# Attention and two mixers on one Trainium2 core: the second chunk's channel units and token products go ahead of the first's last ones, and the first batches' loads and k^T v products are spread

## The chip, the cores and the metric

The program runs on one core of one Trainium2 chip. The time is device microseconds (us) of one execution; three runs of the kernel before gave 1113.26 to 1115.82 us, median 1114.48. Engines: PE (TensorE) does matmuls, DVE (VectorE) and ACT (ScalarE) elementwise work, POOL (GpSimd) small work and some DMA issues, SP (SyncE) issues nearly all DMAs. On each engine instructions run in the order in which they were issued.

## The reference

Eight batches, 8 heads, 576 tokens, head size 64, so the model width is 512. Cut to what matters:

```python
kv  = einsum('bhsd,bhse->bhde', k, v)            # k^T v, no softmax
out = einsum('bhsd,bhde->bhse', q, kv)
x   = out / rms(out) * g_norm                    # heads side by side: [b, 576, 512]

theta = x @ w_theta                              # mixer 1
y = w_tok_r @ (x * cos(theta)) + w_tok_i @ (x * sin(theta))   # over tokens
u = x + y
x = u + relu(u @ w_ch)

h = relu(x^T @ w_tok1) @ w_tok2                  # mixer 2, over tokens: 576 -> 256 -> 576
u = x + h^T
return u + relu(u @ w_ch1) @ w_ch2               # 512 -> 1536 -> 512
```

## The kernel before, in words

**Precision.** Most fp32 products are made of three fp16 products (`mm3`, lines 104 to 106): each operand is split into a high part (ACT) and a low part (DVE: the value minus the high part). Some weights come as 64-bit numbers; `decode` (lines 150 to 158: one ACT copy and three DVE integer operations) makes them fp32 before the split.

**Units.** The tokens are in two chunks, columns 0 to 255 (chunk 0) and 256 to 575 (chunk 1). The work of a batch is cut into units, each one stretch of PE work with ACT and DVE work behind it. In the names the first digit is the chunk, the second the output tile.

- `kv` (L327): k^T v of a batch in two halves (token rows 0 and 1; rows 2, 3 and 4), in the bank kvp; the second half is followed by a copy into kvbd. Each half, when done, issues the loads of the same rows of the next batch's k and v (`load_kv`, L292), since they use the freed buffers.
- a0 to a4, or n0 and n1 when they belong to the batch after next (`attend`, L347): q times kvbd into the bank po, then the norm (ACT L358, DVE L360, POOL, DVE L365) and x. For later batches x is split and transposed by a DMA (L383).
- r0 to r4 (`rotate`): x times w_theta into pt, then L416, L420, sine and cosine (L423 to L425), L428 multiplies by x, L432 and L435 split the result into zh and zl. r4 covers the last 64 tokens; its part of zh comes by a DMA transpose from zt (L480). The buffer cs, which L416 to L435 use, exists twice.
- M00 to M13 (`mix`): 27 matmuls each over zh, zl and wm into py.
- C00 to C13 (`channel`): 12 matmuls each into pr (256 or 320 columns), then DVE L532 adds relu to R, ACT L533 and DVE L540 split the result into xs, and after each second unit SP transposes xs into xt (L544).
- H00 to H11 (`token1`): x^T times w_tok1 into the bank ph; H0x uses chunk 0's xt (6 matmuls), H1x chunk 1's (8). Behind each H1x `split_relu` makes hh and hl.
- T00 to T13 (`token2`): hh, hl times w2 into pu, then DVE L575 adds to R.

**Order.** `run` issues a list of units in program order; a dictionary says what is issued beside (behind) a unit: "a2", "r0", "l" (load the heads of the batch after next), "w" (a step of a weight's load and decode), "k" (a half of `kv`). `go` issues a unit's PE work and lets every unit under way do its next step, so that ACT and DVE work is dealt out behind later units. The list `STEADY` holds the order of batches 2 to 5. `placed`, `lead` and `urgent` say how the scheduler may move instructions. Batch 1 has its own lists because the token units of batch 0 run inside it; batches 6 and 7 have others. After all batches comes the MLP of mixer 2 (`mlp`).

**Start.** Batch 0's q, k, v and w_theta are loaded, then wm of chunk 0 (`mix_weights(0)`), the heads of batch 1, and after batch 0's rotations wm of chunk 1 (`mix_weights(1)`) and w_ch. The weight tiles use staging memory, for wm the buffers that later hold zh and zl. All k^T v products of batches 1 to 7 are made in the start, between batch 0's rotations and beside its M units, before the memory of k and v is given to the decoded weights of the token mixer (w1, w2).

Of the kernel before, what the change touches and what calls it, by code (L numbers as in the profile page):

```python
# [11 lines left out]
F32 = mybir.dt.float32  # L12
# [7 lines left out]
P = 128  # L20
# [8 lines left out]
def attn_mixer_kernel(  # L29
# [4 lines left out]
    nc = tc.nc  # L34
# [4 lines left out]
    NR = S // P  # L39
# [14 lines left out]

    const_ctx, mix_ctx, tok_ctx, front_ctx, start_ctx, stash_ctx = (ExitStack() for _ in range(6))
    const = const_ctx.enter_context(tc.tile_pool(name="const", bufs=1, side="left"))
    zp = mix_ctx.enter_context(tc.tile_pool(name="zp", bufs=2, side="left"))
    mp = mix_ctx.enter_context(tc.tile_pool(name="mp", bufs=1, side="left"))
    fp = front_ctx.enter_context(tc.tile_pool(name="fp", bufs=1, side="right"))
    kp = start_ctx.enter_context(tc.tile_pool(name="kp", bufs=2, side="right"))  # L60
    stg = start_ctx.enter_context(tc.tile_pool(name="stg", bufs=3, side="left"))
# [46 lines left out]

    ident = const.tile([P, P], F32, name="ident")
    make_identity(nc, ident)  # L110
# [185 lines left out]
    for b, o in enumerate(batches):  # L296
        o.b, o.zh, o.kv = b, None, []

# [247 lines left out]
    def token1(o, part, j):  # L546
        b = o.b
        if j == 0 and part == 0:
            o.ph = [bank(f"ph{b}{i}") for i in range(KJ)]
            o.hh = tk[0].tile([P, KJ, DM], F16, tag="hh", name=f"hh{b}", bufs=1)  # L550
            o.hl = tk[0].tile([P, KJ, DM], F16, tag="hl", name=f"hl{b}")
        js = slice(j * P, (j + 1) * P)
        ph = o.ph[j].rearrange("p (k d) -> p k d", k=KD)
        xt = o.x2[part].rearrange("p (k r) d -> p r k d", k=KD)
        low = xt.shape[1] - 2
        for r in range(2):
            wr = 2 * part + r
            nc.tensor.matmul(ph, w1[0][:, wr, js], xt[:, r], start=wr == 0, stop=False)
            nc.tensor.matmul(ph, w1[0][:, wr, js], xt[:, low + r], start=False, stop=False)
            nc.tensor.matmul(ph, w1[1][:, wr, js], xt[:, r], start=False, stop=False)  # L560
        if part:
            nc.tensor.matmul(ph, w1rh[:, js], xt[:, 2], start=False, stop=False)
            nc.tensor.matmul(ph, w1rl[:, js], xt[:, 2], start=False, stop=True)
            yield
            with urgent():
                split_relu(o.hh[:, j, :], o.hl[:, j, :], o.ph[j])
        yield
# [195 lines left out]
    def go(unit, lead=False):  # L763
        advance()
        next(unit)
        (leading if lead else pending).append(unit)

    def advance():

        for units in (leading, pending):  # L770
            for g in list(units):
                try:
                    next(g)
                except StopIteration:
# [26 lines left out]
    prepare(o)  # L801
    extra += mix_weights(0)
    for r in range(1, NR + 1):
# [20 lines left out]
    def run(units, o, nxt, after, also):  # L824
# [21 lines left out]
    loaded = []  # L846
    STEADY = MIX[:6] + CHANNEL[:2] + MIX[6:] + CHANNEL[2:] + TOKEN1 + TOKEN2
    BESIDE = {
        "M00": "a2", "M01": "a3", "M02": "a4 l w", "M03": "r0", "M11": "r1", "M12": "r2",
        "C03": "r4", "C10": "w", "H01": "r3 w n0", "T01": "n1 w", "T12": "w",  # L850
    }
    for b in range(B):
        loaded.clear()
        if b == 0:
            run(MIX, o, nxt, None, {
                "M00": "k w w w", "M01": "k w w w", "M02": "k a0 w", "M03": "k a1 w", "M10": "k a2 k w", "M11": "a3 k w",
                "M12": "a4 r0 k l", "M13": "r1 k",
            })
            after = loaded[0]
            spare(len(extra))  # L860
            flush()
            start_ctx.close()
            wp.append(stash_ctx.enter_context(tc.tile_pool(name="wp", bufs=2, side="right", reuse_waits="tile")))
            tk.append(tok_ctx.enter_context(tc.tile_pool(name="tk", bufs=1, side="left", reuse_waits="tile")))
            extra += [weight_tile(wp[0], w_tok1, w1, j, DT, SW, "w1") for j in range(NR)]
            src, _ = words(w_tok1)
            extra += [weight(wp[0], w_tok1, src[SM:], SR, DT, w1rh[:SR], w1rl[:SR], SW, "w1r")]
            extra += [weight_tile(wp[0], w_tok2, w2, j, S // 2, SW, "w2", col) for j in range(KJ) for col in range(0, S, S // 2)]
            run(CHANNEL, o, nxt, after, {
                "C00": "r2 w", "C01": "r3 w", "C02": "w", "C03": "r4 w", "C10": "w", "C11": "w", "C12": "w", "C13": "w",  # L870
            })
            spare(len(extra))
# [5 lines left out]
        elif b == 1:  # L878
            run(MIX[:4], o, nxt, None, {})
            run(TOKEN1 + TOKEN2, before, None, nxt, {"T00": "n0", "T02": "n1", "T10": "n2 w", "T12": "n3"})  # L880
            run(MIX[4:6] + CHANNEL[:1], o, nxt, None, {"M10": "a4 l"})
            after = loaded[0]
            run(STEADY[STEADY.index("C01"):], o, nxt, after, {
                "C01": "r0", "M12": "r1", "M13": "r2", "C03": "r4", "C10": "w", "H01": "r3 w n0", "T01": "n1 w", "T12": "w",
            })
# [83 lines left out]
```

## Time and profile before

| | kernel before |
|---|---|
| three runs | 1115.82, 1114.48, 1113.26 us |
| the profiled execution's own time | 1117.14 us |
| its span | 1115.4 us |
| PE busy (matmuls) | 1068.9 us, 96% |
| DVE busy | 813.5 us, 73% |
| ACT busy | 567.6 us, 51% |
| mean granted clock of PE | 0.992 |
| moved by DMA | 126.32 MB, mean 113 GB/s |

The span runs from the first to the last instruction that the profiler saw; the execution's own time has a little before and behind it. Busy time says how long an engine had work in flight; what limits a stretch is read from what ended the idle time in it. A wait is put down to what came last. A granted clock of 1.0 is 2.4 GHz on PE, 0.5 is 1.2 GHz.

### The profile page before, as it was taken

What the parts mean: (1) busy time and instruction counts of PE and PEld (TensorE: products, weight loads), DVE (VectorE), ACT (ScalarE), POOL (GpSimd) and SP (SyncE); (2) the same over time, 40 slices, a digit from 0 to 9 for tenths busy, and PEclk for the clock granted to TensorE, in tenths of its full rate; (3) what the DMA queues carried; (4) which work ended last, traced back from release to release, by engine and by line L of the source; (5) the groups of instructions that cost most, each with busy time, mean ns of one, the idle gap of its engine ahead of it and who ended that gap; (6) DMA issues with size and microseconds to landing.
All of it is one profiled execution on the core that took longest, in us unless ns stands there. A gap on an engine that the chain in (4) does not pass through costs nothing.

```text
span 1115.4 us, 21660 instructions
## 1 busy us (share of the span) xinstructions
PE 1068.9 (96%) x8884; PEld 812.2 (73%) x8884; DVE 813.5 (73%) x1483; ACT 567.6 (51%) x970; POOL 189.7 (17%) x259
## 2 busy tenths in 40 slices
PE   4789989999999999989999999999999999999998
PEld 4467667676766767657777777777777777777776
DVE  5877787889788886888745585848677685758584
ACT  3754654737456464565522544536264544446361
POOL 3203005262443624435000000000000000000000
PEclk9889999999999999999999999999999999999999
DMA  9899447383754837546274702020110102020101
GB/s 302 240 308 287 115 110 183 81 216 99 171 150 106 221 95 170 142 106 141 39 264 103 267 11 75 8 79 1 43 43 29 59 11 76 12 75 1 44 1 43
DMA packets 147859, 126.32 MB, mean 113 GB/s; under 512 B 93296, under 2 KB 123120, under 8 KB 147760
## 3 DMA queue, kind: packets, MB, share of 16 engines
q1 hardware_dynamic: 142384, 104.49, 35.4%
q0 software_dynamic: 5376, 20.45, 5.1%
q8 instruction: 69, 1.13, 0.4%
q14 instruction: 30, 0.25, 0.1%
HBM read 74.25 MB, written 29.88 MB: 93 GB/s over the span
## 4 chain that ended last, share of the span: by engine, by line
PE 63%; DVE 14%; DMA 9%; ACT 6%; issue 2%; POOL 2%; SPq 2%; DVEq 0%; ACTq 0%
PE na L104 4%; PE pa L104 4%; PE pa L106 4%; PE pa L105 4%; PE na L106 4%; PE na L105 4%; DMA xt<-xs 3%; PE py L104 3%; PE py L106 3%; PE py L105 3%; DVE zl L435 2%; PE pc L106 2%; PE pc L105 2%; PE pc L104 2%; PE nc L105 2%
## 5 line engine op out<-in xcount | busy, mean ns | idle before, releaser
L104 PE MATMUL py<-wmh,zh 128*128 128x320 f16 (+1 forms) x576 | 166.4, 289 | 2.6 <-ACT zh L432 2.0
L105 PE MATMUL py<-wml,zh 128*128 128x320 f16 (+1 forms) x576 | 166.3, 289 | 0.0
L106 PE MATMUL py<-wmh,zl 128*128 128x320 f16 (+1 forms) x512 | 147.9, 289 | 1.6 <-DVE zl L435 1.6
L106 PE MATMUL na<-gh,wbl 128*128 128x288 f16 x384 | 109.3, 286 | 0.0
L105 PE MATMUL pa<-o,wah 128*128 128x288 f16 x384 | 109.2, 286 | 0.0
L105 PE MATMUL na<-gl,wbh 128*128 128x288 f16 x384 | 109.1, 286 | 0.0
L104 PE MATMUL pa<-o,wah 128*128 128x288 f16 x384 | 108.4, 286 | 0.0
L106 PE MATMUL pa<-o,wal 128*128 128x288 f16 x384 | 107.8, 286 | 0.0
L104 PE MATMUL na<-gh,wbh 128*128 128x288 f16 x384 | 106.0, 286 | 0.2
L648 DVE TENSOR_TENSOR gl<-sum,gh 128x1152 f16<-128x1152 f32 x48 | 65.1, 1356 | 21.9 <-ACT gh L647 21.9
L105 PEld LDWEIGHTS <-wbh 128*128 128x128 f16 x672 | 65.7, 98 | 17.7 <-issue 1.0
L104 PEld LDWEIGHTS <-wah 128*128 128x128 f16 x672 | 65.8, 98 | 16.6
L105 PEld LDWEIGHTS <-wah 128*128 128x128 f16 x672 | 65.8, 98 | 16.6
L106 PEld LDWEIGHTS <-wbl 128*128 128x128 f16 x672 | 65.7, 98 | 16.6
L106 PEld LDWEIGHTS <-wal 128*128 128x128 f16 x672 | 65.8, 98 | 16.6
L104 PEld LDWEIGHTS <-wbh 128*128 128x128 f16 x672 | 65.7, 98 | 16.6
L106 PE MATMUL pr<-uh,wcl 128*128 128x256 f16 (+1 forms) x256 | 73.1, 286 | 0.3 <-DVE wcl L180 0.3
L105 PE MATMUL pr<-ul,wch 128*128 128x256 f16 (+1 forms) x256 | 73.1, 286 | 0.0
L104 PE MATMUL pr<-uh,wch 128*128 128x256 f16 (+1 forms) x256 | 73.0, 286 | 0.0
L104 PEld LDWEIGHTS <-zh 128*128 128x128 f16 x576 | 57.0, 99 | 19.0 <-ACT zh L432 2.3
L647 ACT ACTIVATE gh<-sum 128x1152 f16<-128x1152 f32 x48 | 55.6, 1158 | 25.5 <-DVE sum L695 25.5
L105 PEld LDWEIGHTS <-zh 128*128 128x128 f16 x576 | 57.0, 99 | 15.7
(309 smaller groups left out, 2866.5 us busy)
## 6 DMA issues: line engine op xcount, KB each, us to landing
c<-u2d SPq DMA_DIRECT2D x32, 288.0 KB, 4.5
out<-c SPq DMA_DIRECT2D x64, 144.0 KB, 1.8
q<-in_q SPq DMA_DIRECT2D x7, 1152.0 KB, 7.0
k<-in_k SPq DMA_DIRECT2D x24, 256.0 KB, 5.7
v<-in_v SPq DMA_DIRECT2D x24, 256.0 KB, 6.1
wa_r<-in_w_ch SPq DMA_DIRECT2D x24, 256.0 KB, 3.6
wb_r<-in_w_ch SPq DMA_DIRECT2D x24, 256.0 KB, 3.8
wad<-wa POOLq DMA_DIRECT2D x24, 224.0 KB, 2.4
```

The costliest lines, as they stand in the source:

```text
L104: nc.tensor.matmul(acc, ah, bh, start=first and i == 0, stop=False, **more)
L105: nc.tensor.matmul(acc, ah, bl, start=False, stop=False, **more)
L106: nc.tensor.matmul(acc, al, bh, start=False, stop=last and i == n - 1, **more)
L435: place(nc.vector.tensor_tensor(zl[:, at, :], cs, zh[:, at, :], ALU.subtract))
L647: nc.scalar.activation(h.hi[:, 3:], h.s, AF.Copy)
L648: nc.vector.tensor_tensor(h.lo[:, 3:], h.s, h.hi[:, 3:], ALU.subtract)
```

## The change

It has three parts.

1. The order of a steady batch. Before: M00 to M11, C00, C01, M12, M13, C02, C03, C10 to C13, H00, H01, H10, H11, T. After: M00 to M13, C00, C01, C10 to C13, C02, C03, H10, H11, H00, H01, T. `token1` may now begin with either chunk: the bank's first product starts it and the second closes it. r4 is issued beside C01, and r3, n0 and n1 beside C03 (before: r4 beside C03, r3 and n0 beside H01, n1 beside T01).
2. The start. wm of chunk 1 is loaded and decoded ahead of k and v of batch 2; `settle` lets the decode of chunk 0 end first. The two halves of k^T v of batch 1 stand beside r3 and r4 of batch 0, and the twelve halves of batches 2 to 7 one behind each of batch 0's eight M units and of C00 to C03. Batch 1's attend units stand beside M00 to M10, its rotations r0 to r2 beside M10 to M12 (before: M12, M13, C00). The memory of k and v (`heads_ctx`) is given back after C03, so w1 and w2 are loaded and decoded beside C10 to C13, two steps a unit.
3. Batch 1 follows the new steady order from M11 on, with r0 to r2 beside M11, M12 and M13.

```diff
-    kp = start_ctx.enter_context(tc.tile_pool(name="kp", bufs=2, side="right"))
+    kp = heads_ctx.enter_context(tc.tile_pool(name="kp", bufs=2, side="right"))
...
-        if j == 0 and part == 0:
+        if o.ph is None:
             o.ph = [bank(f"ph{b}{i}") for i in range(KJ)]
...
+        parts = []
         for r in range(2):
             wr = 2 * part + r
-            nc.tensor.matmul(ph, w1[0][:, wr, js], xt[:, r], start=wr == 0, stop=False)
-            nc.tensor.matmul(ph, w1[0][:, wr, js], xt[:, low + r], start=False, stop=False)
-            nc.tensor.matmul(ph, w1[1][:, wr, js], xt[:, r], start=False, stop=False)
+            parts += [(w1[0][:, wr, js], xt[:, r]), (w1[0][:, wr, js], xt[:, low + r]), (w1[1][:, wr, js], xt[:, r])]
         if part:
-            nc.tensor.matmul(ph, w1rh[:, js], xt[:, 2], start=False, stop=False)
-            nc.tensor.matmul(ph, w1rl[:, js], xt[:, 2], start=False, stop=True)
+            parts += [(w1rh[:, js], xt[:, 2]), (w1rl[:, js], xt[:, 2])]
+        again = j in o.half
+        for i, (w, x) in enumerate(parts):
+            nc.tensor.matmul(ph, w, x, start=not again and i == 0, stop=again and i == len(parts) - 1)
+        o.half.add(j)
+        if again:
             yield
...
+    def settle(units):
+
+        while any(u in pending or u in leading for u in units):
+            advance()
...
     nxt = load_heads(1)
-    for r in range(NR + 1):
+    for r in range(NR - 1):
         go(rotate(o, r))
-        if r == 1:
-            go(kv(nxt, 0))
-            go(kv(nxt, 1))
-        elif r > 1:
-            go(kv(*products.pop(0)))
+    settle(narrow)
+    extra += mix_weights(1)
+    for r in range(NR - 1, NR + 1):
+        spare()
+        go(rotate(o, r))
+        go(kv(nxt, r - NR + 1))
+        spare()
+    spare(len(extra))
     flush()
-    extra += mix_weights(1)
...
-    STEADY = MIX[:6] + CHANNEL[:2] + MIX[6:] + CHANNEL[2:] + TOKEN1 + TOKEN2
+    STEADY = MIX + CHANNEL[:2] + CHANNEL[4:] + CHANNEL[2:4] + TOKEN1[2:] + TOKEN1[:2] + TOKEN2
     BESIDE = {
         "M00": "a2", "M01": "a3", "M02": "a4 l w", "M03": "r0", "M11": "r1", "M12": "r2",
-        "C03": "r4", "C10": "w", "H01": "r3 w n0", "T01": "n1 w", "T12": "w",
+        "C01": "r4", "C12": "w", "C03": "r3 n0 n1 w", "T01": "w", "T12": "w",
     }
...
-                "M00": "k w w w", "M01": "k w w w", "M02": "k a0 w", "M03": "k a1 w", "M10": "k a2 k w", "M11": "a3 k w",
-                "M12": "a4 r0 k l", "M13": "r1 k",
+                "M00": "a0 k", "M01": "a1 k w", "M02": "a2 k w", "M03": "a3 k w", "M10": "a4 k r0 w", "M11": "r1 l k", "M12": "r2 k", "M13": "k",
...
+            run(CHANNEL[:4], o, nxt, after, {"C00": "k", "C01": "r3 k", "C02": "k", "C03": "r4 k"})
+            heads_ctx.close()
...
-            run(CHANNEL, o, nxt, after, {
-                "C00": "r2 w", "C01": "r3 w", "C02": "w", "C03": "r4 w", "C10": "w", "C11": "w", "C12": "w", "C13": "w",
-            })
+            run(CHANNEL[4:], o, nxt, after, {"C10": "w w", "C11": "w w", "C12": "w w", "C13": "w"})
...
-            run(MIX[4:6] + CHANNEL[:1], o, nxt, None, {"M10": "a4 l"})
+            run(MIX[4:5], o, nxt, None, {"M10": "a4 l"})
             after = loaded[0]
-            run(STEADY[STEADY.index("C01"):], o, nxt, after, {
-                "C01": "r0", "M12": "r1", "M13": "r2", "C03": "r4", "C10": "w", "H01": "r3 w n0", "T01": "n1 w", "T12": "w",
+            run(STEADY[STEADY.index("M11"):], o, nxt, after, {
+                "M11": "r0", "M12": "r1", "M13": "r2", "C01": "r4", "C12": "w", "C03": "r3 n0 n1 w", "T01": "w", "T12": "w",
             })
```

What the change does to the order of DVE is shown at the end of batch 3's channel units; before, the last units there are C12 and C13 (pr312, pr313 and their output xs312; zl4 and zt4 are the next batch's rotations):

```order
L532 SCALAR_TENSOR_TENSOR R3_2601<-pr312_4204,R3_2601 128x320
L435 TENSOR_TENSOR zl4_3811<-cs42_4024,zh4_3810 128x2x512
L540 SCALAR_TENSOR_TENSOR xs310_4157<-R3_2601,xs310_4157 128x256
L540 SCALAR_TENSOR_TENSOR xs310_4157<-R3_2601,xs310_4157 128x64
L532 SCALAR_TENSOR_TENSOR R3_2601<-pr313_4223,R3_2601 128x320
L540 SCALAR_TENSOR_TENSOR xs312_4203<-R3_2601,xs312_4203 128x256
L540 SCALAR_TENSOR_TENSOR xs312_4203<-R3_2601,xs312_4203 128x64
L475 TENSOR_TENSOR zt4_4151<-cs44_4150,zt4_4151 128x512
L540 SCALAR_TENSOR_TENSOR xs312_4203<-R3_2601,xs312_4203 128x256
L540 SCALAR_TENSOR_TENSOR xs312_4203<-R3_2601,xs312_4203 128x64
```

The same place on DVE after the change, where C02 and C03 (pr302, pr303, xs302) follow C13:

```order
L532 SCALAR_TENSOR_TENSOR R3_2576<-pr312_4162,R3_2576 128x320
L467 SCALAR_TENSOR_TENSOR cs44_4112<-R4_3418,cs44_4112 128x4x64 x2
L532 SCALAR_TENSOR_TENSOR R3_2576<-pr313_4191,R3_2576 128x320
L435 TENSOR_TENSOR zl4_3811<-cs42_3975,zh4_3810 128x2x512
L540 SCALAR_TENSOR_TENSOR xs312_4161<-R3_2576,xs312_4161 128x256
L540 SCALAR_TENSOR_TENSOR xs312_4161<-R3_2576,xs312_4161 128x64
L532 SCALAR_TENSOR_TENSOR R3_2576<-pr302_4208,R3_2576 128x256
L475 TENSOR_TENSOR zt4_4113<-cs44_4112,zt4_4113 128x512
L532 SCALAR_TENSOR_TENSOR R3_2576<-pr303_4226,R3_2576 128x256
L540 SCALAR_TENSOR_TENSOR xs312_4161<-R3_2576,xs312_4161 128x256
L540 SCALAR_TENSOR_TENSOR xs312_4161<-R3_2576,xs312_4161 128x64
L540 SCALAR_TENSOR_TENSOR xs302_4207<-R3_2576,xs302_4207 128x256 x2
```

The additions L532 of two more channel units now stand ahead of the last two L540, behind which SP transposes xs312 for H10 and H11.

On SP, in the start, the loads before run from batch 1's last rows of k and v on (wm13r and wm17r are single tiles of chunk 1's wm, wmh1 the pairs wm10 and wm11 in one of zh's buffers):

```order
L292 DMA k14_374<-in_k 96x512
L292 DMA v14_376<-in_v 96x512
L205 DMA wm13r_864<-in_w_mix 128x640
L205 DMA wm17r_868<-in_w_mix 128x640
L314 DMA q1_378<-in_q 128x4x576
L316 DMA q1_378<-in_q 128x4x64
L292 DMA k20_459<-in_k 128x512
```

And after, the same stretch of SP's queue:

```order
L292 DMA v14_376<-in_v 96x512
L205 DMA wmh1_456<-in_w_mix 128x2x640 x2
L205 DMA wm13r_646<-in_w_mix 128x640
L205 DMA wm17r_651<-in_w_mix 128x640
L314 DMA q1_378<-in_q 128x4x576
L316 DMA q1_378<-in_q 128x4x64
L292 DMA k20_515<-in_k 128x512
L292 DMA v20_517<-in_v 128x512
L292 DMA k21_519<-in_k 128x512
L292 DMA v21_521<-in_v 128x512
L205 DMA wml1_457<-in_w_mix 128x2x640
```

The two pairs in wmh1, which stood behind all of batch 2's k and v, are now ahead of them, and the pair in wml1 is in their middle. On DVE the decode of these two pairs is issued about r0 and r1 of batch 0 (cs00, cs01) after the change:

```order
L158 SCALAR_TENSOR_TENSOR wm10v_473<-wmh1_456,wm10v_473 128x640
L420 SCALAR_TENSOR_TENSOR cs00_405<-cs00_405,pt00_392 128x512
L156 TENSOR_SCALAR wm11v_532<-wm11v_532 128x640
L214 SCALAR_TENSOR_TENSOR wml_115<-wm08v_390,wmh_114 128x256
L214 SCALAR_TENSOR_TENSOR wml_115<-wm10v_473,wmh_114 128x2x320
L157 SCALAR_TENSOR_TENSOR wm11v_532<-wmh1_456,wm11v_532 128x640
L420 SCALAR_TENSOR_TENSOR cs01_430<-cs01_430,pt01_417 128x512
L69 SCALAR_TENSOR_TENSOR xt04_335<-px4_431,xt04_335 128x512
L158 SCALAR_TENSOR_TENSOR wm11v_532<-wmh1_456,wm11v_532 128x640
L428 TENSOR_TENSOR cs00_405<-cs00_405,x00_240 128x1024
L214 SCALAR_TENSOR_TENSOR wml_115<-wm11v_532,wmh_114 128x2x320
L428 TENSOR_TENSOR cs01_430<-cs01_430,x01_254 128x1024
```

Before, the L420 of cs00 and cs01 and the L428 of cs00 stood next to one another there, and the decode of wm10 came behind zl of r1.

## Rows read from the trace of the kernel before

**Rows 1.** The page's first block: busy us, share of the span, instructions.

```profile
PE 1068.9 (96%) x8884; PEld 812.2 (73%) x8884; DVE 813.5 (73%) x1483; ACT 567.6 (51%) x970; POOL 189.7 (17%) x259
```

**Rows 2.** Waits of PE, whole span: us in total, times, longest.

```profile
PE ph L558 <- DMA xt<-xs: 8.4, 8, 1.3
PE pu L104 <- DVE R L575: 2.3, 5, 0.5
```

**Rows 3.** Waits of PE in 44 to 160 us.

```profile
PE kvp L327 <- DMA v<-in_v: 6.6, 6, 4.0
PE py L104 <- ACT zh L432: 2.0, 1, 2.0
PE py L106 <- DVE zl L435: 1.6, 1, 1.6
PE py L104 <- DMA zh<-zt: 0.7, 1, 0.7
```

**Rows 4.** Windows: length, busy of five engines, PEclk, DMA share, GB/s.

```profile
46.00:115.00 69.00, 62.44 (x828) 47.27 (x825) 51.65 (x88) 36.12 (x67) 10.54 (x10) 0.95 1.02 293
64.00:69.00 5.00, 4.95 (x35) 3.74 (x36) 4.97 (x9) 3.85 (x7) 0.00 (x0) 0.50 1.06 290
144.00:147.00 3.00, 3.00 (x17) 2.13 (x16) 3.00 (x11) 2.09 (x5) 0.00 (x0) 0.52 0.31 87
```

**Rows 5.** Timeline of PE, batch 3: start, duration, instruction, [idle before].

```profile
344.13 0.30 PE L106 MATMUL pr<-uh,wcl 128*128 128x320 f16 x1
344.27 0.38 PE L558 MATMUL ph<-xt,w1h 128*128 128x512 f16 x1
...
349.45 1.05 PE L347 MATMUL po<-kvbd,q 128*128 128x128 f32 x8
351.81 0.39 PE L558 MATMUL ph<-xt,w1h 128*128 128x512 f16 x1 [1.31 <-DMA xt<-xs]
...
355.71 1.06 PE L347 MATMUL po<-kvbd,q 128*128 128x128 f32 x8
356.60 0.27 PE L104 MATMUL pu<-w2h,hh 128*128 128x256 f16 x1
356.71 0.27 PE L105 MATMUL pu<-w2l,hh 128*128 128x256 f16 x1
...
361.84 0.30 PE L104 MATMUL pu<-w2h,hh 128*128 128x320 f16 x1 [0.45 <-DVE R L575]
```

**Rows 6.** Timeline of DVE at the same place in batch 3.

```profile
344.56 1.22 DVE L435 TENSOR_TENSOR zl<-cs,zh 128x1024 f16<-128x1024 f32 x1
...
346.17 0.49 DVE L532 SCALAR_TENSOR_TENSOR R<-pr,R 128x320 f32<-128x320 f32 x1
```

**Rows 7.** Timeline of SP's queue at the same place.

```profile
346.31 3.26 SPq L544 DMA_TRANSPOSE xt<-xs  x2
```

**Rows 8.** Timelines of PE and DVE: batch 1's r3, last matmul, L420, zl.

```profile
126.20 0.38 PE L106 MATMUL pt<-wth,xt 128*128 128x512 f16 x1
...
135.31 0.68 DVE L420 SCALAR_TENSOR_TENSOR cs<-cs,pt 128x512 f32<-128x512 f32 x1
...
141.78 1.23 DVE L435 TENSOR_TENSOR zl<-cs,zh 128x1024 f16<-128x1024 f32 x1
```

**Rows 9.** Timeline of DVE: zl of batch 0's r0, decode of wm10.

```profile
48.91 1.22 DVE L435 TENSOR_TENSOR zl<-cs,zh 128x1024 f16<-128x1024 f32 x1 [0.79 <-ACT zh L432]
...
60.53 0.82 DVE L157 SCALAR_TENSOR_TENSOR wm10v<-wmh,wm10v 128x640 int32<-128x640 int32 x1
```

**Rows 10.** Timeline of PE: first half of batch 3's k^T v.

```profile
64.05 0.80 PE L327 MATMUL kvp<-v,k 128*64 128x64 f32 x10 [3.97 <-DMA v<-in_v]
```

**Rows 11.** Timeline of SP: first and last loads of w1 and w2.

```profile
122.76 0.52 SPq L143 DMA_DIRECT2D w_0r<-in_w_tok  x1
...
157.03 2.81 SPq L143 DMA_DIRECT2D w_1r<-in_w_tok  x2
```

**Rows 12.** The page's DMA issues: count, KB each, median us to landing.

```profile
v<-in_v SPq DMA_DIRECT2D x24, 256.0 KB, 6.1
```

More of the change, by code (lines that the diff above doesn't have):

```diff
@@ L53, in attn_mixer_kernel @@
     dr = ctx.enter_context(tc.tile_pool(name="dr", bufs=1, space=DRAM))
-    const_ctx, mix_ctx, tok_ctx, front_ctx, start_ctx, stash_ctx = (ExitStack() for _ in range(6))
+    const_ctx, mix_ctx, tok_ctx, front_ctx, heads_ctx, start_ctx, stash_ctx = (ExitStack() for _ in range(7))
     const = const_ctx.enter_context(tc.tile_pool(name="const", bufs=1, side="left"))
@@ L106, in mm3 @@
             nc.tensor.matmul(acc, al, bh, start=False, stop=last and i == n - 1, **more)
-    ident = const.tile([P, P], F32, name="ident")
+    ident = stg.tile([P, P], F32, name="ident", bufs=1)
     make_identity(nc, ident)
@@ L296, in attn_mixer_kernel @@
     for b, o in enumerate(batches):
-        o.b, o.zh, o.kv = b, None, []
+        o.b, o.zh, o.kv, o.ph, o.half = b, None, [], None, set()
     def load_heads(b):
@@ L801, in attn_mixer_kernel @@
     prepare(o)
-    extra += mix_weights(0)
+    narrow = mix_weights(0)
+    extra += narrow
     for r in range(1, NR + 1):
@@ L862, in attn_mixer_kernel @@
             start_ctx.close()
+            tk.append(tok_ctx.enter_context(tc.tile_pool(name="tk", bufs=1, side="left", reuse_waits="tile")))
+            run(CHANNEL[:4], o, nxt, after, {"C00": "k", "C01": "r3 k", "C02": "k", "C03": "r4 k"})
+            heads_ctx.close()
             wp.append(stash_ctx.enter_context(tc.tile_pool(name="wp", bufs=2, side="right", reuse_waits="tile")))
-            tk.append(tok_ctx.enter_context(tc.tile_pool(name="tk", bufs=1, side="left", reuse_waits="tile")))
             extra += [weight_tile(wp[0], w_tok1, w1, j, DT, SW, "w1") for j in range(NR)]
```

## The prediction

> **What bounds the kernel now.** I read the page's first block, then the waits of TensorE (PE), then the timelines at the places that those waits name. PE is busy for nearly all of the span [rows 1], so a change of order can win only PE's waits, and time lost at the lower clock. Over the whole span two of the waits lie in the repeated part: the first token product (ph) waits eight times for the transposed channel output xt, 8.4 us in all, and the second (pu) five times, 2.3 us [rows 2]. The others lie in the start, 44 to 160 us: k^T v (kvp) waits there 6.6 us for v, and batch 1's first mixes (py) 2.0 + 1.6 + 0.7 = 4.3 us for rotated rows [rows 3]. The granted clock is about one half in 64 to 69 and 144 to 147 [rows 4]: PE ran at 1.2 GHz, not 2.4, and the same work at full rate takes half as long, so 2.5 and 1.5 us are lost. The start loses 6.6 + 4.3 + 2.5 + 1.5 = 14.9 us, the repeated part 10.7. Nothing that the change touches can win more than 25.6 us. The MLP's half of the span and batches 6 and 7 keep their order.
>
> **Part 1, steady order (batches 1 to 5).** Before, the second chunk's product H10 is issued behind C13, H00, H01, r3 and n0. In batch 3 C13 ends where H00 starts, 344.27; H00, H01 and r3 take 5.18 (344.27 to 349.45; each of the two 2.59, twelve rows of 0.216), n0 0.89 by the spacing of a po block (355.71 to 356.60), and H10 starts at 351.81 after a wait of 1.31 [rows 5]. So its operand comes 351.81 - 344.27 = 7.54 us after C13. After, C13 is followed by C02 and C03 (2 x 12 matmuls at 0.11, the spacing of 356.60 to 356.71, is 2.62), r3 2.59, n0 and n1 2 x 0.89: 6.99 us, against 2.59 + 2.59 + 0.89 = 6.07 before. Cover grows by 0.92.
>
> Of the 8.4 us, five waits are such second-chunk waits; the longest is 1.3 [rows 2], and I read 6.0 us in them (0.97 to 1.31 each), the other three, 2.4 us, at H00. The five fall to 1.20 - 0.92 = 0.28 each. But VectorE (DVE) now has two additions L532 of C02 and C03, at most 0.49 each [rows 6], ahead of the last xs, which the transpose needs. They arrive while DVE would do its other work (zl L435, 1.22) and not all of it delays xs: I add 0.3, bounds 0 and 0.98. Left: 5 x 0.58 = 2.9, won 3.1. The transposes stand on SP one behind another, two of them 3.26 us in their issue [rows 7]; their number is unchanged.
>
> H00's operand came, before, 4 x 12 x 0.14 = 6.7 us after C03 (spacing 344.13 to 344.27 [rows 5]) plus at most 1.3, thus 8.0. Now it has r3 2.59, n0 and n1 1.78 and H10, H11 (16 x 0.216 = 3.5) ahead, 7.8 us plus what H10 still waits: no wait, 2.4 won. The pu wait goes, since T00's bank is no longer the one that the last H frees late: 2.3 won, bounds 0 and 2.3. n1 stands 3 units earlier; its ScalarE and DVE work moves with it, and PE waits for none of it before T. Were the bank of n0 or n1 to hold up T10, up to 0.45 a batch comes back, the price of today's pu wait [rows 5]. Sum: -3.1 - 2.4 - 2.3 = -7.8, bounds -10.7 and 0.
>
> **Part 2, batch 1's first mixes.** Batch 1's rotation r3 has its product finished at 126.2, yet its addition L420 runs at 135.31 and its zl at 141.78 [rows 8]: 15 us behind, because r0 to r3 were issued close together and share two buffers. Now r0 to r2 stand two M units earlier (2 x 27 x 0.14 = 7.6 us) and no first-token weight is decoded beside C00 to C03. zl of r3 comes at least 7 us earlier, around 135, before M00 reaches that row. 4.3 us and the slow stretch behind it, 1.5, go: -5.8, bounds -5.8 and 0.
>
> **Part 3, batch 0's start.** The decode of the weights wm10 and wm11 now stands ahead of r0's chain on DVE. Each is four operations of at most 0.82, 3.3 us a pair and 6.6 both; an idle 0.79 stands before r0's zl today [rows 9], which the decode fills. With r1's 1.2 us product also moved ahead, r0's zl would end at 50.13 + 6.6 + 1.2 - 0.8 = 57.1 if all of it delayed the chain, and at 50.13 if none did; I take 54, since DVE has to wait there for ScalarE and for pt01 anyway. r2's chain can't begin before r0's buffer is free, and then takes 7.7 us, as r3's did from L420 to the end of zl (135.31 to 143.01 [rows 8]), or more where decodes stand between: near 65, with 2 to 3 us for these. PE was free today at 64.05 - 3.97 = 60.1 [rows 10]; without three product halves (about 1.1 us each) and their other waits (6.6 - 4.0 - 0.3) it reaches M00 near 54.5. Up to 65 it has rows r0 and r1 of M00 to M02 (36 x 0.11 = 4.0), three po blocks (2.7) and k^T v of batch 2 (2.6), 9.3 us: it waits 1.2 there, about 1.5 for r3's zl, and some 2 for kvbd1 and for k20, which is loaded only when kvp1 is done. New waits: 5 us, bounds 2.6 and 8.
>
> The halves of k^T v move behind the units, so that each has more time to land: the near three had waits of up to 3.97 [rows 10]. The last ones stand beside short C units (1.31 us); the half of batch 7 then has some 5 to 7 us against a landing that took 6.1 in the median for v [rows 12]. I take 2.5 us of v waits, bounds 0 and 6.6. The last weights w1 and w2 now load only at C10: before, their loads ran from 122.76 to 157.03 [rows 11], 34 us, and they have about 24 now; SP is not held by batch 0's other work then. I take 0.75, bounds 0 and 10. Stretches at the lower clock: 1.5, bounds 0 and 4. The start costs 5 + 2.5 + 0.75 + 1.5 = 9.75 against 14.9 today: -5.2 with part 2 in it.
>
> On the clock the row shows 0.50 right behind the 3.97 us wait [rows 4, 10]. The Trainium skill, "TensorE: Matmul & The Clock Gate", section "HAM oscillation — how this bites in real kernels", says that idle gaps throttle the engine again and the work behind them is paid at half rate. By that rule the 5 + 2.5 us of waits would cost another 2.5 beyond what I count, start -2.7 and the time 1103.9. The trace agrees at this stall and behind the py waits of 2.0 and 1.6 (0.52 in 144 to 147), and shows no such stretch behind the waits under 1 us; the new waits are several short ones, so I keep 1.5.
>
> **Sum.** -7.8 - 5.2 = -13.0. The profiled execution took 1117.14 (span 1115.4); 1104.1 is its time after. The median of the runs is 2.66 below it: about 1101.4 us.
>
> **The rivals.**
> R1, the start wins nothing: 14.9 us are paid again, by v waits. For it speaks that 293 GB/s were already moved in 46 to 115 [rows 4], and that wm10 and wm11 (1.3 MB) are now ahead of all of batch 2's k and v on SP. The Trainium skill, "DMA: Bandwidth & Descriptors", section "Queues, rings and completion order", has the descriptors of one ring start in order, so that k and v would stand behind these weights. Against it: k20 can't be issued before kvp1 has freed its buffer, by which time 1.3 MB at 293 GB/s (4.5 us) have landed. Time: 1117.14 - 7.8 - 2.66 = 1106.7.
> R2, H10 keeps its price because DVE, not the transposes, sets when the last xs is written: zl and the two L532 fill all of the gained 0.92. Then the steady part wins 4.7, and the time is 1104.5. Part 1 as a whole failing is 1109.2.
> R3, slower: every k^T v half of batches 2 to 7 waits for its v, 12 halves. A half's buffers are freed by the half two before it, and SP issues up to six loads between; if a load takes longer than two units, each half pays. The six waits of today come to 1.1 each, the longest 3.97 [rows 3, 10]; near the former, 2.2 a half, it is 26.4 us. The other terms of the start hide in these waits, and today's 6.6 + 5.8 and the steady 7.8 are won: 26.4 - 20.2 = +6.2, 1120.7. It decides from 20.2 / 12 = 1.7 us a half. Against it: an M unit with its half and po block takes 2.95 + 1.1 + 0.9, two of them 10 us.
> R4, nothing: with 1.7 us a half, or w1 and w2 late by 10 us and the second-chunk waits kept, 1114.
>
> **How the numbers follow.** Forecast 0.57 (its own range 1096 to 1106), R1 0.18, R2 or all of part 1 failing 0.09, R3 0.09, R4 0.07. A measurement of this kernel tells 0.2%, 2.2 us, from no change. Faster: 0.57 + 0.18 + 0.09, and a little of R4: 0.85; same 0.06; slower 0.09. The range 1095 to 1111 takes in R1, R2 and part 1 failing; it leaves out R3, R4 and a sum at all its good ends.
>
> **What would show it.** In the waits of PE: ph L564 (the new line of L558) five times at about 0.6, none at H00, no pu wait; no py wait for batch 1; instead py waits for zl and zh rows in 55 to 72, and kvp waits of 1 to 3 us only at the last halves. M00 to M03 of batch 1 in about 11.8 us at the full clock. It is wrong if kvp waits exceed 6.6 in the start (R1, above 20: R3), if ph keeps over 5 us (R2), or if py or pr waits for w1, w2, wm12 or wm13 appear between M10 and the first T.

## The result and the profile after

The changed kernel took 1120.49 us (median of 20 runs, 1112.93 to 1125.77), the kernel before 1114.39 (20 runs, 1111.73 to 1117.66): slower by 6.1 us, ratio 1.0051 with the interval 1.0036 to 1.0067. The forecast was 1101.4 with the range 1095 to 1111, so even its sign was wrong. The runs of the changed kernel are also more than twice as far apart as those of before; the mean granted clock of its three longest was 0.985 to 0.986, of its three shortest 0.991 to 0.992.

The profiled execution was its shortest run, 1112.93 (span 1110.9). The same kernel was therefore profiled again; that execution took 1122.51 (span 1120.7). Waits of PE in the first one, whole span (us in total, times, longest):

```profile
PE kvp L327 <- DMA v<-in_v: 14.6, 7, 9.9
PE ph L564 <- DMA xt<-xs: 7.5, 3, 3.7
PE ph L564 <- DVE ss L360: 6.1, 2, 3.6
PE pu L104 <- ACT hh L72: 0.7, 1, 0.7
PE pr L105 <- DVE ul L510: 0.5, 1, 0.5
PE py L106 <- DVE zl L435: 0.3, 1, 0.3
```

Against [rows 2, 3]: the py waits of batch 1 are gone, and so is the pu wait for R; but ph, the first token product, waits 13.6 us instead of 8.4. There are five of these waits, one in each of batches 1 to 5, all at H10. (Two are put down to `ss L360`, the instruction of DVE that came last; DVE's order below shows that the operand xt is what is late.)

Batches 1 to 5 are best seen in one window from the end of batch 0's token products (first M unit behind them) to the end of batch 5's. Columns: window, length, busy of PE, PEld, DVE, ACT, POOL, then PEclk. Before:

```profile
170.87:502.00 331.13, 320.43 (x2499) 230.36 (x2497) 272.02 (x487) 186.67 (x335) 141.76 (x191) 1.00 0.58 147
```

The changed kernel, second profile:

```profile
165.37:507.37 342.00, 325.73 (x2499) 232.22 (x2497) 275.91 (x491) 187.27 (x335) 141.90 (x191) 0.98 0.59 143
```

The stretch begins 5.5 us earlier: that is the start's gain in this execution. It is 10.9 us longer: PE's idle time rose from 10.7 to 16.3 us (+5.6), and its busy time, over the same 2499 matmul records, by 5.3. The same work takes longer because some of it ran at 1.2 GHz; windows of this profile and of the first one:

```profile
420.00:424.00 4.00, 3.38 (x9) 1.22 (x10) 3.56 (x5) 2.04 (x3) 3.92 (x5) 0.50 0.95 201
```

```profile
274.30:278.00 3.70, 3.63 (x11) 1.43 (x12) 3.00 (x4) 1.77 (x3) 3.62 (x6) 0.65 0.97 224
484.00:488.00 4.00, 3.73 (x11) 1.44 (x12) 3.26 (x5) 2.06 (x3) 3.92 (x6) 0.62 1.01 137
```

In the first profile (start of the stretch 9.9 us earlier) the stretch took 336.59 us, 5.4 us less: 3.3 us of it are busy time, since two such windows lie in it and not three, and 2.1 idle time. So the time of this kernel depends also on how many of its stalls are followed by half clock, which is in line with the scatter of its runs.

Why H10 waits is seen in batch 3, first profile. Timeline of PE; 335.43 is the start of C02, thus C13's end, and 338.05 the start of r3, C03's end:

```profile
335.29 0.30 PE L106 MATMUL pr<-uh,wcl 128*128 128x320 f16 x1
335.43 0.27 PE L104 MATMUL pr<-uh,wch 128*128 128x256 f16 x1
...
338.05 0.38 PE L104 MATMUL pt<-wth,xt 128*128 128x512 f16 x1
...
344.96 0.38 PE L564 MATMUL ph<-xt,w1h 128*128 128x512 f16 x1 [2.38 <-DMA xt<-xs]
```

H10's operand comes 344.96 - 335.43 = 9.53 us after C13; in the kernel before it was 7.54 [rows 5]. Batch 3 is one of the milder cases: in batches 2 and 5, whose waits are 3.67 and 3.62 us, it comes 10.8 us after C13, against 7.5 before. DVE at the same place of batch 3:

```profile
336.37 0.48 DVE L532 SCALAR_TENSOR_TENSOR R<-pr,R 128x320 f32<-128x320 f32 x1
336.77 0.75 DVE L467 SCALAR_TENSOR_TENSOR cs<-R,cs 128x256 f32<-128x256 f32 x2
337.44 0.48 DVE L532 SCALAR_TENSOR_TENSOR R<-pr,R 128x320 f32<-128x320 f32 x1
337.84 1.22 DVE L435 TENSOR_TENSOR zl<-cs,zh 128x1024 f16<-128x1024 f32 x1
338.97 0.55 DVE L540 SCALAR_TENSOR_TENSOR xs<-R,xs 128x256 f16<-128x256 f32 x2
339.44 0.42 DVE L532 SCALAR_TENSOR_TENSOR R<-pr,R 128x256 f32<-128x256 f32 x1
339.77 0.68 DVE L475 TENSOR_TENSOR zt<-cs,zt 128x512 f16<-128x512 f32 x1
340.37 0.42 DVE L532 SCALAR_TENSOR_TENSOR R<-pr,R 128x256 f32<-128x256 f32 x1
340.71 1.22 DVE L540 SCALAR_TENSOR_TENSOR xs<-R,xs 128x256 f16<-128x256 f32 x4
```

And SP's queue:

```profile
341.32 2.85 SPq L544 DMA_TRANSPOSE xt<-xs  x2
```

There is no idle time in the rows of DVE. C13's product is ready at 335.43, its addition L532 runs at 337.44, and the two L540 that xt waits for are the first half of the group at 340.71: about 341.3, 5.8 us behind C13. SP issues the transposes at that moment, so it is DVE that they wait for. DVE before, beside [rows 6]:

```profile
344.16 0.48 DVE L532 SCALAR_TENSOR_TENSOR R<-pr,R 128x320 f32<-128x320 f32 x1
...
346.56 0.56 DVE L540 SCALAR_TENSOR_TENSOR xs<-R,xs 128x256 f16<-128x256 f32 x2
347.03 0.69 DVE L475 TENSOR_TENSOR zt<-cs,zt 128x512 f16<-128x512 f32 x1
347.63 0.56 DVE L540 SCALAR_TENSOR_TENSOR xs<-R,xs 128x256 f16<-128x256 f32 x2
```

There the last L540 ended at 348.2, 3.9 us behind C13's end at 344.27 [rows 5]. The L532 of C13 itself is no later now than before (2.0 and 1.9 us behind C13), but that hides the lag: zl (L435), which stood ahead of it, now stands behind it. The L532 of C12 shows it: 0.1 us ahead of C13's end before (344.16), 0.9 behind it now (336.37).

From the end of r2's product to C13's end both orders have the same units; DVE's busy time (fifth column) in these 14.21 us, before and after:

```profile
330.06:344.27 14.21, 14.21 (x149) 11.09 (x148) 13.16 (x26) 10.09 (x20) 5.01 (x6) 1.00 0.33 78
321.22:335.43 14.21, 14.21 (x149) 11.08 (x148) 13.44 (x24) 10.80 (x22) 4.00 (x6) 1.00 0.13 32
```

So DVE does not work less there; it comes into the stretch with more left to do. What differs lies ahead: C00 and C01 stood between r1 and r2, and from the end of r1's product to that of r2's PE took 8.9 us before and takes 6.3 now.

### The profile page after: what moved, and what is told of

It reads as the page before. It is cut to its first block, busy times and chain, and to the rows that moved or that the text cites. A ratio compares the mean times of both kernels' runs of the same rounds, so it can differ in the third digit from the quotient of the medians.

```text
span 1110.9 us, 21682 instructions
## 1 busy us (share of the span) xinstructions
PE 1067.7 (96%) x8884; PEld 813.1 (73%) x8884; DVE 815.1 (73%) x1483; ACT 567.6 (51%) x970; POOL 195.1 (18%) x259
## 4 chain that ended last, share of the span: by engine, by line
PE 68%; DVE 13%; DMA 7%; POOL 4%; ACT 4%; issue 3%; SPq 1%; ACTq 0%; DVEq 0%; POOLq 0%
PE na L104 4%; PE pa L106 4%; PE pa L105 4%; PE pa L104 4%; PE na L106 4%; PE na L105 4%; PE ph L564 4%; PE py L104 3%; PE py L105 3%; PE py L106 3%; PE pc L106 2%; PE pc L105 2%; PE pc L104 2%; PE nc L104 2%; PE nc L105 2%
## 5 line engine op out<-in xcount | busy, mean ns | idle before, releaser
L104 PE MATMUL py<-wmh,zh 128*128 128x256 f16 (+1 forms) x576 | 165.3, 287 | 0.0
L105 PE MATMUL py<-wml,zh 128*128 128x256 f16 (+1 forms) x576 | 165.3, 287 | 0.0
L507 ACT ACTIVATE uh<-R 128x256 f16<-128x256 f32 (+1 forms) x64 | 28.0, 440 | 97.8 <-DVE R L506 97.7
L362 POOL TENSOR_TENSOR ri<-ss,mhalf 128x8 f32<-128x8 f32 x40 | 73.8, 1845 | 2.9
```

The source lines that it names most:

```text
L104: nc.tensor.matmul(acc, ah, bh, start=first and i == 0, stop=False, **more)
L105: nc.tensor.matmul(acc, ah, bl, start=False, stop=False, **more)
L362: nc.gpsimd.tensor_tensor(ri, ss, mhalf, ALU.pow)
L507: lead(nc.scalar.activation(uh[:, dt, :], u, AF.Copy, scale=1.0 / SW))
```

## The experiments

Two theories were stated at first. T1: DVE, which works in order, runs late behind the channel units of the new steady order; H10 stalls, and some stalls bring half clock; the start wins what its profile shows. T2: the start's gain is not steady. T3 and T5 came later: that the DMA transposes, or PE's own order, set the H10 wait. Each ratio is to the kernel before, timed beside the run.

**The start alone** (e1_start): the changed kernel with the steady order of before.

```diff
-    STEADY = MIX + CHANNEL[:2] + CHANNEL[4:] + CHANNEL[2:4] + TOKEN1[2:] + TOKEN1[:2] + TOKEN2
+    STEADY = MIX[:6] + CHANNEL[:2] + MIX[6:] + CHANNEL[2:] + TOKEN1 + TOKEN2
...
-        "C01": "r4", "C12": "w", "C03": "r3 n0 n1 w", "T01": "w", "T12": "w",
+        "C03": "r4", "C10": "w", "H01": "r3 w n0", "T01": "n1 w", "T12": "w",
...
```

> The changed start with the steady order of the kernel before (batch 1's own lists too). T1 (VectorE runs late behind the channel units in the new steady order, H10 waits 1.5 to 3.7 us a batch, and each such stall may be followed by a stretch at half clock; the start itself wins what its profile shows, about 10 us): 1103 to 1106, runs as close together as those of before (6 us from lowest to highest), PE waits of ph and pu as before (10.7 us). T2 (the start's gain is not steady: its waits for v and its slow stretches vary from run to run, and the steady part costs only the 3 us that the one profile shows): 1111 to 1118, runs spread over 10 us or more.

Measured: 1106.92 us (1106.16 to 1108.40), ratio 0.9938 (0.9926 to 0.9950). The start is worth -6.9 us, a little less than T1 had it, and the runs lie close together. Its waits of PE for ph and pu are those of before:

```profile
PE ph L564 <- DMA xt<-xs: 6.2, 6, 1.3
PE pu L104 <- DVE R L578: 2.2, 5, 0.5
```

**The steady order alone** (e2_steady): the kernel before with the diff's STEADY, BESIDE, batch 1 lists and token1.

> The changed steady order (and token1 that begins with the second chunk, batch 1's lists) with the start of the kernel before. T1: 1122 to 1130, wide spread, granted clock 0.984 to 0.989, ph waits of 13 to 15 us in five to six places. T2: 1115 to 1118, spread as before.

Measured: 1124.33 (1123.38 to 1127.09), ratio 1.0098 (1.0082 to 1.0113): +10.5 us. Both runs speak for T1 and against T2, but for the scatter: the runs of e2, with H10 waits of 3.1 to 3.6 us in batches 2 to 5, lie within 3.7 us, where T1 expected a wide spread. -6.9 + 10.5 is +3.6, against +6.1 for both parts together, so 2.5 us are not accounted for by adding. Waits of PE:

```profile
PE ph L564 <- DVE ss L360: 10.5, 3, 3.6
PE ph L564 <- DMA xt<-xs: 4.6, 2, 3.1
```

**r4 behind the last xs** (e3_r4late), **more cover behind C13** (e4_cover):

```diff
-        "C01": "r4", "C12": "w", "C03": "r3 n0 n1 w", "T01": "w", "T12": "w",
+        "C12": "w", "C03": "r3 n0 n1 w", "H10": "r4", "T01": "w", "T12": "w",
...
```

> The changed kernel with rotation r4 issued beside H10 instead of C01, so its 1.9 us of VectorE work (L456, two L467, L475) stand behind the last xs. T1: the H10 wait falls by 1.5 to 2 us in each batch, to 0 to 1.9, slow stretches mostly go, time 1107 to 1113. T3 (the transposes and the weight loads on the DMA queue set when xt lands, not VectorE): waits within 0.5 us of the 1.5 to 3.7 of the changed kernel, time 1117 to 1123.

```diff
-    STEADY = MIX + CHANNEL[:2] + CHANNEL[4:] + CHANNEL[2:4] + TOKEN1[2:] + TOKEN1[:2] + TOKEN2
+    STEADY = MIX[:3] + MIX[4:] + MIX[3:4] + CHANNEL[4:] + CHANNEL[:4] + TOKEN1[2:] + TOKEN1[:2] + TOKEN2
...
-        "M00": "a2", "M01": "a3", "M02": "a4 l w", "M03": "r0", "M11": "r1", "M12": "r2",
+        "M00": "a2", "M01": "a3", "M02": "a4 l w r0", "M11": "r1", "M12": "r2",
...
```

> The changed kernel, in batches 2 to 5 with M03 behind M13 and the channel units as C10 to C13, C00 to C03: H10 is then reached 2.6 us later after C13, plus 1.4 us of r4, which stands beside C01 as before. T1: 10.9 us of cover against the 10.8 us that H10's operand took: waits of 0 to 1 us in batches 2 to 5, no slow stretch there, time 1104 to 1110. T2: the steady part wins 6 us at most and the unsteady start stays: 1111 to 1118.

e3 was a miss: 1123.43 (1122.32 to 1125.29), ratio 1.0087 (1.0073 to 1.0102), H10 waits of 3.6 to 4.4 us in batches 2 to 5. In batch 3 of its profile DVE stood still shortly before the channel units (C00 starts there at 327.6):

```profile
318.02 1.09 DVE L265 SCALAR_TENSOR_TENSOR wa<-wa_s,wa 128x896 f16<-128x896 f32 x1 [3.42 <-ACT wa L263]
...
322.84 1.09 DVE L265 SCALAR_TENSOR_TENSOR wa<-wa_s,wa 128x896 f16<-128x896 f32 x1 [1.60 <-DMA wad<-wa]
```

The instruction at the head of its queue (the low half of an MLP weight) waited for ACT and for a transfer, and all behind it waited too: 5 us lost, more than the 1.9 that moving r4 gave. In the changed kernel the same two L265 waited 0.1 us together. Nor was 1.9 the gain: r4's 1.4 us of PE work, in which DVE could catch up, left the place ahead of C10 too, so that some 0.5 remain, an estimate from the two figures. e4 was as T1 had it, 1109.34 (1103.99 to 1115.86), ratio 0.9965 (0.9949 to 0.9981): no ph wait over 0.6 us in batches 2 to 5, though pr and pu waits of 0.5 to 1.0 took a part of the place. Only the time is at the upper end of what was expected.

**Rotations earlier** (e5_early, and with the steady order of before e6_start_early):

```diff
-        "M00": "a2", "M01": "a3", "M02": "a4 l w", "M03": "r0", "M11": "r1", "M12": "r2",
-        "C01": "r4", "C12": "w", ...
+        "M00": "a2 r0", "M01": "a3", "M02": "a4 l w r1", "M10": "r2", "M12": "r4",
+        "C12": "w", ...
```

> The changed kernel, in batches 2 to 5 with the next batch's rotations earlier: r0 beside M00, r1 beside M02, r2 beside M10, r4 beside M12 (there VectorE is busy only half of the time: 6.0 of 12 us in 354 to 366). T1 (VectorE is the bound from M03 to the last xs and is late with it; only work taken out of that stretch, or more PE work behind C13, helps): the last xs comes 3 us or more earlier relative to C13, H10 waits under 0.8 us in batches 2 to 5, no slow stretch there, time 1103 to 1109. T3 (the transposes on the queue set it): H10 waits stay at 2.4 to 3.7 us, time 1117 to 1123.

> The changed start with the steady order of before, and the next batch's rotations earlier as in the run beside it (r0 M00, r1 M02, r2 M10, r4 M12). T1: VectorE is less behind at the channel units, the ph waits of before (0.4 to 1.3 us at H00 and H10) fall to about half, 1102 to 1106. T3: ph waits unchanged, 1106 to 1108. If the earlier rotations make PE wait for x (a1, a2 not through): po, pt waits in M00 to M10 and 1108 or more.

e5: 1106.39 (1105.16 to 1110.53), ratio 0.9932 (0.9910 to 0.9955): 14 us faster than the changed kernel. The H10 waits of batches 2 to 5 were 2.25, 1.48, 1.08 and 1.68, not under 0.8 as expected, and the first of them was followed by half clock (below): half of the mechanism. e6: 1117.05 (1114.79 to 1121.48), ratio 1.0027 (1.0013 to 1.0042): the third case of its expectation, pt waits of 1.9 to 2.0 us for r1's x in each batch, since x of r1 comes from n1, which stands later in that order (beside T01).

**Cover and early rotations together** (e7_cover_early, e9_cover_fixed, e12_cover_r4): e4's order with r0 beside M00, r1 beside M02, and r2, r4 at M10, M12; at M11, M13; at M11, M03. The last two also have n0 and n1 ahead of r3, C12's "w" beside H01, and batch 1's rotations earlier.

> The order with C10 to C13 ahead of all of C00 to C03 and M03 behind M13, together with the earlier rotations. T1: no ph wait over 0.3 us in batches 2 to 5, the pr wait for uh (0.6 to 1.0 today) and the pu wait for hl smaller since VectorE is not behind, 1102 to 1107; batch 1 as in the run without the earlier rotations. T3: as that run, 1107 to 1112.

> The changed start; batches 2 to 5 with M03 behind M13 and the channel units as C10 to C13, C00 to C03, as in the cover run, and with the rotations early enough for VectorE and late enough for x: r0 M00, r1 M02, r2 M11, r4 M13; n0 and n1 ahead of r3 beside C03; the weight step of C12 beside H01, so that its loads don't stand ahead of the transposes on SP. Batch 1 with r0 to r2 one unit earlier, r4 at M13, the same n0, n1, r3. Cover behind C13 is 4 x 1.31 + 2.59 + 1.78 = 9.6 us, against the 8.5 that H10's operand took with early rotations. T1: no ph wait over 0.2 us in batches 2 to 5, below 1 in batch 1, pr waits for uh under 0.5 since VectorE is not behind, pu waits under 0.5; 1098 to 1103. If the waits only change their place (pr, pu, pt): 1104 to 1110.

> As the last cover run, with r4 of batches 2 to 5 beside M03 instead of M13: its 3.0 to 3.5 us waits came because x of a4, issued at M02, is transposed only 7 units later. One unit (2.95 us) more covers most of it. T1: no wait over 0.6 us in batches 2 to 5, no slow stretch there, 13 us less than that run's profile: 1099 to 1104. If the wait only moves to C10 (pr for uh or ul): 1103 to 1109.

All three missed: 1125.14 (ratio 1.0081, 1.0049 to 1.0113), 1115.91 (1.0027, 1.0012 to 1.0042) and 1112.88 (0.9984, 0.9972 to 0.9996). Each took the H10 wait of over 2 us away and put others in its place: pt waits of 2.8 to 3.3 us in e7 for x of r2, of 2.4 to 3.5 in e9 at r4, and in e12 pr, ph and pt waits of 0.4 to 1.2. The units of x, rotation and channel are a chain, and a rotation put ahead of what feeds it makes PE wait there.

**DVE relieved by another engine** (e8_pool):

```diff
-            place(nc.vector.tensor_tensor(zl[:, at, :], cs, zh[:, at, :], ALU.subtract))
+            if b > 1 and r in (1, 2):
+                nc.gpsimd.tensor_tensor(zl[:, at, :], cs, zh[:, at, :], ALU.subtract)
+            else:
+                place(nc.vector.tensor_tensor(zl[:, at, :], cs, zh[:, at, :], ALU.subtract))
```

> The changed kernel with the subtraction L435 of r1 and r2 (batches 2 and up) on GpSimd instead of VectorE; nothing else moves. It takes 2.4 us a batch from VectorE ahead of the last xs. T1: H10 waits fall by 1.5 to 2.4 us in batches 2 to 5, to 0 to 1.5, and the slow stretches behind them go: 1106 to 1113. T3: waits and time as the changed kernel, 1117 to 1123. If GpSimd slows VectorE down while both work, the gain is smaller: 1112 to 1117.

Measured: 1121.52 (1113.89 to 1132.42), ratio 1.0058 (1.0035 to 1.0081), H10 waits of 3.7 to 4.2: no relief. POOL's and DVE's timelines in batch 3 (L543 and L535 are L540 and L532 here):

```profile
335.07 2.13 POOL L436 TENSOR_TENSOR zl<-cs,zh 128x1024 f16<-128x1024 f32 x1 [2.16 <-ACT zh L432]
...
342.16 2.19 POOL L436 TENSOR_TENSOR zl<-cs,zh 128x1024 f16<-128x1024 f32 x1 [2.83 <-ACT zh L432]
```

```profile
335.85 1.63 DVE L543 SCALAR_TENSOR_TENSOR xs<-R,xs 128x256 f16<-128x256 f32 x1 [0.95 <-ACT xs L536]
...
342.28 0.48 DVE L535 SCALAR_TENSOR_TENSOR R<-pr,R 128x320 f32<-128x320 f32 x1
342.68 2.08 DVE L543 SCALAR_TENSOR_TENSOR xs<-R,xs 128x256 f16<-128x256 f32 x2
```

The L543 that came while POOL worked ended 0.3 us behind it, after 1.63 us instead of 0.43, and the pair took 2.08 instead of 0.55; L535, one of whose inputs is in PSUM, kept its 0.48. The Trainium skill, "SBUF — State Buffer", section "🔬 SBUF: two separate sides", says that GpSimd and a VectorE operation with two SBUF inputs share one pair of ports as an exclusive lock, so that the second blocks for the whole instruction. The trace agrees.

**DVE relieved by leaving work out** (e10_relief, and e13_r4late_relief with r4 beside H10): the three integer operations L156 to L158 of the MLP weights' decode are left out. L156 shifts the whole word, so those weights have quite other values, not only other last bits as the expectation has it; PE uses them only in the MLP.

```diff
         yield
+        if short:
+            return
         place = placed if wp else lambda ins: ins
```

> The changed kernel with the three integer operations of VectorE left out in the decode of the MLP's weights (24 tiles, L156 to L158, 0.42 + 0.69 + 0.69 = 1.8 us each; the weights' last bits are then missing). One such decode stands in VectorE's stretch ahead of the last xs in each of batches 2 to 5. No instruction of another engine is left out or moved in the program. T1: the last xs and H10 come up to 1.8 us earlier, waits of 0.5 to 2.2 us, fewer slow stretches, time 1108 to 1115. T3 (DMA sets it): waits 1.5 to 3.7 and 1117 to 1123 as in the changed kernel.

> The run with r4 beside H10, with the three integer operations L156 to L158 of the MLP weights' decode left out as in the relief run. With the decode in, VectorE stood 3.4 and 1.6 us in front of L265 (the weight's low half, which waits for GpSimd and ScalarE) just before the channel units, which used up the 1.9 us that r4's moving gave. T1 (what counts is how far VectorE is behind at C13, by work or by a wait at the head of its queue): no wait of VectorE over 1 us at L265 there, H10 waits at most 1.5, down to 0.3; 1101 to 1107. T5 (r4's work doesn't matter; PE's own order sets the H10 wait): waits as in the run with r4 late, 3.5 us and more, or 1.4 to 1.6 plus the 1.4 of r4's products, 3 us; 1110 or more.

e10: 1105.49 (1104.32 to 1105.67), ratio 0.9926 (0.9914 to 0.9938), 15 us below the changed kernel although no PE instruction moved in the program. Its batches 1 to 5:

```profile
163.60:490.22 326.62, 319.06 (x2498) 230.73 (x2496) 239.44 (x425) 187.54 (x335) 128.35 (x191) 1.00 0.58 151
```

DVE's 36 us less there gave PE 8.7 us less idle time and 6.7 us less busy time than in the second profile of the changed kernel. The H10 waits are 1.4 to 1.6 us each. The expected time, 1108 to 1115, was too high, since no slow window was left in batches 1 to 5. Of the 17.2 us between the two spans 15.4 lie in these batches, where PE doesn't touch the weights concerned. e13: 1107.73 (1106.47 to 1110.96), ratio 0.9956 (0.9940 to 0.9973), H10 waits 1.5 to 2.6: below T5's 3 us, above T1's 1.5. DVE no longer stands in front of L265 there. But the waits are longer than e10's 1.4 to 1.6, so moving r4 won nothing by itself.

**The weight loads on SP** (e14_early_w): e5 with C12's "w" beside H01 in batches 2 to 5. In e5's SP timeline two loads stand between the second chunk's transposes (the 5.69 covers one of chunk 0 and one of chunk 1):

```profile
333.08 5.69 SPq L544 DMA_TRANSPOSE xt<-xs  x2
338.82 1.20 SPq L143 DMA_DIRECT2D wa_r<-in_w_ch  x2
340.13 3.62 SPq L544 DMA_TRANSPOSE xt<-xs  x2
```

> The run with early rotations, in batches 2 to 5 with the weight step of C12 beside H01: its two loads then don't stand on SP between the two transposes of the second chunk (0.7 us and 0.5 us there). Now that VectorE is no longer behind, SP's queue should show: H10 waits in batches 2 to 5 fall by about 0.8, from 1.1 to 2.3 to 0.3 to 1.5; 1101 to 1105. If the loads were not on the path: waits and time as that run, 1105 to 1108.

Measured: 1111.13 (1108.39 to 1115.33), ratio 0.9980 (0.9966 to 0.9994). PE's waits in that run:

```profile
PE pt L104 <- DMA xt<-xs: 10.1, 7, 2.3
PE ph L564 <- DMA xt<-xs: 1.6, 1, 1.6
```

The ph waits of batches 2 to 5 are gone altogether (the 1.6 is batch 1's); but the rotations r2 and r4 of those batches wait 10.1 us for the transposes of x, and the time is worse than e5's. The loads were on H10's path: in batch 2 of e5 SP issues the transposes 0.8 us after xs of C12 and C13 is complete (270.45 and 269.65), with the two loads in between, in e14 0.1 us after it (268.57 and 268.50). The waits of 1.1 to 2.3 us fell by more than that; xs itself came 1.1 us earlier there behind C13, and whether PE's new waits for x gave DVE this time is not shown. The weight step that moved has work on DVE too: in batch 3 the last low half of x (L382) runs 12.9 us behind M10's start, against 8.3 in e5, with one more L265 ahead of it. So x's transposes are late at least in part because DVE is; what share the moved loads have on SP is not shown.

**The changed kernel again** (e11_after_again):

> The changed kernel again, for a second profile. The first one was of its shortest run (1112.93, clock 0.991) while the median is 1120.5. T1 (a stall of 2.4 us or more at H10 is sometimes followed by a stretch at half clock): a run of about 1120 shows H10 waits of the same size and half-clock stretches behind four or five of them, not two; the start is within 2 us of the first profile's. T2: the start is longer by 5 us or more.

Measured: 1122.51 and 1118.66, the kernel before 1113.55 beside it. Its H10 waits in the profile are 1.83, 3.67, 2.77, 3.62 and 3.64; half-clock windows follow the three longest, not four or five; the start is 4.4 us longer than in the first profile, between the two expectations. So T1's clock term is there, and the start also varies by some us.

Of the versions that leave nothing out, e1_start and e5_early are the fastest, 1106.9 and 1106.4, not told apart by these runs; e4_cover (1109.3) too is clear of both kernels.

## Why the prediction was wrong

**The failed step** is in part 1, the price of DVE's work ahead of the last xs: "I add 0.3, bounds 0 and 0.98. Left: 5 x 0.58 = 2.9, won 3.1." It counts the two added L532 alone and takes the rest of DVE's work there to be as far along at C13 as before: a growth of DVE's lag stands at nothing. Measured: 9.53 instead of 7.54 us from C13 to H10's operand in batch 3, so +2.0, and +3.3 in batches 2 and 5; H10 waits of 13.6 and 15.5 us in the two profiles instead of 2.9. Of the 2.0 the two L532 are 0.67 (0.33 and 0.34 from their starts to the next ones), inside their bounds; the other 1.3 or so is work that DVE had done by C13's end before, and still has ahead of it now. The other side of the sum was right: H10 is reached 344.96 - 2.38 - 335.43 = 7.15 us after C13, 6.99 forecast.

The trace of before already showed DVE with no idle time at that place. That such a lag sets the wait is shown: in e10 DVE work is left out, in e5 it is done earlier, and both shorten the wait; e14 shows what comes next in e5, two weight loads on SP between the transposes. Why the lag grew is in part argued: C00 and C01 no longer stand between r1 and r2, and C02 and C03 went behind C13. So from r1 to C13 PE has 2.6 us less to do, and DVE loses that time, while only two channel units' own work leaves DVE there; no run moved these units alone.

**The term that was missing** is the clock in batches 1 to 5. In the two profiles of the changed kernel and that of e2 all nine H10 waits of 3.0 us or more were followed by windows with a granted clock of 0.50 to 0.67, and the six of 1.5 to 2.8 us by none; busy time in the second profile is 5.3 us longer. The length of the wait alone does not decide it: in e5 a wait of 2.25 us was followed by half clock, in e3 one of 2.09 (0.57), and in e9 one of 3.36 was not. The windows behind the waits in e5 and e9:

```profile
274.80:278.80 4.00, 4.00 (x11) 1.44 (x12) 3.91 (x6) 2.73 (x5) 3.18 (x5) 0.58 0.95 223
253.80:257.80 4.00, 4.00 (x73) 3.73 (x74) 3.94 (x6) 4.00 (x8) 1.28 (x3) 1.00 0.17 64
```

The prediction weighed the rule on idle gaps (the Trainium skill, "TensorE: Matmul & The Clock Gate", section "HAM oscillation — how this bites in real kernels") for the start alone, because it saw no long waits in batches 1 to 5. The trace agrees with that rule in the nine cases.

**Right:** H00's waits (2.4) and the pu waits for R (2.3) are gone. For H00 the sum leaves out r4's 1.4 us between C03 and C10 (before, 336.35 to 344.27 is 7.9 us, not 6.7), and H00 is reached, with H10's wait, only 10.4 us after C03 in batch 3 (338.05 to 348.41), not 7.8; that the forecast cover alone would have done is not shown. M00 to M03 of batch 1 have no wait. The start won 6.9 us alone, against 5.2 forecast, with its parts off: the wait of batch 0's M units for zl and kvbd was 1.6 and 1.9 us in the two profiles (1.3 of it put down to issue) instead of 5, those for v 3.1 and 4.8 us instead of 2.5. No wait of PE is put down to a late w1 or w2 (0.75 forecast); at the first T it waits 0.7 and 0.2 us for hh.

**The rivals.** R1 and R3 did not happen: no half of k^T v waited over 1.7 us in the two profiles. That R3's time, 1120.7, lies beside the measured 1120.5 is luck: its 26.4 us of waits for v were 3.1 and 4.8. R2, "zl and the two L532 fill all of the gained 0.92", named the right engine and instructions, but stopped at today's price; it did not ask whether DVE would get later than today. The rival that ended on the slower side was placed in the start, where DMA limits; the loss came in the steady part.

Open: why the parts do not add up (2.5 us), and what makes the scatter: e2 and e3, whose H10 waits in batches 2 to 5 are 3.1 us or more, have runs within 3.7 and 3.0 us, the changed kernel within 12.8.

## What to carry to other kernels

Where an engine that feeds the critical one is nearly always busy in a stretch, its lag can grow with every unit that is moved out of the way of its other work: work out when its queue would get through the new sequence, rather than adding the moved instructions to today's lag. Price a stall on TensorE with the stretch at half clock that may follow it. Before moving a wait's cause on one queue, list what else moves with it and what will stand behind it: the weight step taken out of one transpose's way brought its DVE work in front of x.

## What the runs showed of the hardware

GpSimd's 128x1024 subtraction took 2.1 to 2.2 us and stretched a VectorE operation with two SBUF inputs from 0.43 to 1.63 us; moving work there gave nothing. A wait at the head of VectorE's in-order queue, for a weight that nobody needed soon, took 3.4 us from the work behind it.
